# Chunked attention, Fourier mixing and MLP on one core: the first batch's up-projection begun token tile by token tile

## The chip, the cores and the metric

The kernel runs on one core of one Trainium2 chip. The metric is the device time of the whole program in microseconds (us); where several runs are compared, the median counts. All arithmetic is in 32-bit floats; the MLP's weights come in as 64-bit floats and are rounded to 32 bits on the chip.

## The reference

Eight batches of 576 tokens, eight heads of 64. Attention is taken within chunks of 64 tokens; then a two-dimensional Fourier transform whose real part is added, a norm, and an MLP of width 2048 with a Relu.

```python
scores = scale * np.matmul(q_c, k_c.transpose(0, 1, 2, 4, 3))   # per chunk of 64 tokens
scores = scores - np.max(scores, axis=-1, keepdims=True)
attn = np.exp(scores)
attn = attn / (np.sum(attn, axis=-1, keepdims=True) + 1e-09)
x = np.matmul(attn, v_c)                                        # then (B, S, H * D) = (8, 576, 512)
X = np.fft.fft(np.fft.fft(x, axis=1), axis=2)
u = x + np.real(X)
mu = np.mean(u, axis=-1, keepdims=True)
var = np.mean((u - mu) ** 2, axis=-1, keepdims=True)
un = (u - mu) / np.sqrt(var + 1e-06)
out = u + np.maximum(un @ w_ch1, 0.0) @ w_ch2                   # w_ch1 (512, 2048), w_ch2 (2048, 512)
```

## The kernel before, in words

The order of the work on each engine is the order in which the program writes it; nothing is rescheduled. An instruction waits for the data that it needs and for the buffer that it writes to be given up by its last reader, and whatever is written later for the same engine waits behind it.

**Start.** The first batch (b = 0) goes alone, with functions of its own. attention_early does the attention of its five token tiles (four full ones and a rest tile that it shares with batch 1). fourier_early then does its Fourier mixing in three parts, divided by yields: first the products with the sequence tables into z and the middle row mid (L741, L744), which are copied to zf (L751 to L759) and zr (L761 to L767); then the products with the dimension tables into early_xp (L771); then, for each of two pairs of token tiles (low and high), the addition to x (L785, L788, L789), the mean and variance (means: L633 and L634 on VectorE, L637 and L638 on ScalarE, which give rstd), the normalisation (normed, L819 to L825) and the transposition by TensorE and ScalarE (turned: four transposes L329, then the copy L838 into unT). normed works on ScalarE for the first tile (L823, with a shift made by L819 on VectorE) and on VectorE for the other three (L825). keep_warm issues products of a constant tile into a buffer that nobody reads (idle, L1143).

**Rounding the weights.** The weights come in as 32 pieces: four groups of four for w_ch1 (512 hidden features, that is four feature tiles, by 128 input features each, with the group outermost), then those of w_ch2; the pieces are numbered in this order. round_weight(i) does the head of piece i and the tail of piece i - 1. The head ("h" below) is two masks on VectorE (L305, L308) and three steps on ScalarE: fraction (L299) and exponent (L302, L303). The tail ("t") is three steps on VectorE (L317, L318, L319), of which L317 needs L299 and L318 needs L303; it then gives the raw buffer free, and the load of a later piece is issued on SP's queue (L284). Seven raw buffers are filled from the start. round_next calls round_weight for the next piece; attention_early calls it twice, the second time with put_off, a list into which the ScalarE steps are put instead of being issued; the main program issues them after the first part of fourier_early. A third call follows after fourier_early.

**The main loop.** After that, the MLP of batch group after batch group runs step by step, and after each step the loop writes a share of the next batch's attention and Fourier work ("sides"), and then round_next, twice in each of the first four steps. For the first group, up_first walks over four groups f of four feature tiles; for each it takes four PSUM buffers up and sums over the four input pieces kk, with one yield after each kk; after the last kk each up goes through a Relu on ScalarE into h1 (L939). So the step of f and kk needs exactly its own weight piece, the pieces being numbered in the same order. In the third step's share the loop writes the transposes of batch 1's first q and k; in the fourth's, after the first four Relus, its scores (sc, L380), their maximum (L393) and the subtraction (L395).

**PSUM.** ps_t has two buffers of one bank (transposes, z), ps_a one buffer of two banks (the second half of z, and the scores sc), ps_f four buffers of one bank (idle, the two early_xp, mid, later up). A buffer of a pool is taken over when all that used it is through.

Of the kernel before, what the change touches and what calls it, by code (L numbers as in the profile page):

```python
# [8 lines left out]
FP32 = mybir.dt.float32  # L9
# [7 lines left out]
def kernel(  # L17
# [265 lines left out]
            free.remove(fit[0])  # L283
            nc.sync.dma_start(out=raw(i).rearrange("p f r -> p (f r)"), in_=pieces[i][1].bitcast(U32))  # L284

    def round_weight(i, later=None):

        if i < len(pieces):
            w, t = pieces[i][0], raw(i)
            lo, hi, wi = t[:, :, 0], t[:, :, 1], w.bitcast(U32)
            p = power[i] = three_p.tile([128, 512], U32, tag="o", name="power")

            def fraction(w=w, wi=wi):
                nc.scalar.activation(out=w, in_=wi, func=ACTF.Copy, scale=2.0 ** -20, bias=1.0)  # L299

            def exponent(p=p):
                nc.scalar.activation(out=p, in_=p, func=ACTF.Relu, scale=-1.0, bias=top[:, 0:1])  # L302
                nc.scalar.activation(out=p, in_=p, func=ACTF.Relu, scale=-8.0, bias=top[:, 1:2])  # L303

            nc.vector.tensor_scalar(wi, hi, 0x000FFFFF, None, ALU.bitwise_and)  # L305
            if later is None:
                fraction()
            nc.vector.tensor_scalar(p, hi, 0x7FF00000, None, ALU.bitwise_and)  # L308
            if later is None:
                exponent()  # L310
            else:
                later += [fraction, exponent]
        if 0 < i <= len(pieces):
            w, t = pieces[i - 1][0], raw(i - 1)
            lo, hi = t[:, :, 0], t[:, :, 1]
            p = power.pop(i - 1)
            nc.vector.scalar_tensor_tensor(w, lo, 2.0 ** -52, w, ALU.mult, ALU.add)  # L317
            nc.vector.scalar_tensor_tensor(p, hi, 0x80000000, p, ALU.bitwise_and, ALU.bitwise_or)  # L318
# [208 lines left out]
    def attention_early():  # L527

        lo, hi = first[0], first[1] - 1

        def ready(n):
            if n == at[LO, 0, 1]:
                shift_early(0)
            if n == at[HI, 0, 1]:
                fold(0, 1)
            if n == at[HI, 0, 0]:
                fold(0, 0)
            if n + 3 > hi:
                load_v(n + 3)

        att_T(lo)
        att_S(lo)
        for n in range(lo, hi + 1):
            if n < hi:
                att_T(n + 1)
            softmax(n)
            if n > lo:
                att_V(n - 1)
                ready(n - 1)
            if n < hi:  # L550
                att_S(n + 1)
            if n in (lo, hi):
                keep_warm(1)
            att_P(n)
        shift_early(1)
        fold(0, NM)
        keep_warm(1)
        att_V(hi)
        ready(hi)
        keep_warm(6)  # L560
        turn_tables()
        round_next()
        round_next(put_off)

    def attention(b):

# [156 lines left out]
    def fourier_early():  # L723
# [12 lines left out]
        for i in order:  # L736
            at_ = {"start": i == order[0], "stop": i == order[-1], "skip_group_check": True}
            for T in range(4):
                p = slice(0, 128) if i < NM else slice(T % 2 * CH, T % 2 * CH + CH)
                d0_ = T * HQ if i < NM else T // 2 * HQ  # L740
                nc.tensor.matmul(out=z[T][:, 0:NQ], lhsT=pm[i][p, d0_:d0_ + HQ], rhs=tk[p, i, T // 2], **at_)  # L741
            p, d0_ = (slice(0, 128), DM) if i < NM else (slice(CH, 128), 2 * HQ)
            for r, (c0, c1) in enumerate(mids):
                nc.tensor.matmul(  # L744
                    out=mid[32 * r:32 * r + 1, 0:c1 - c0], lhsT=pm[i][p, d0_:d0_ + 1], rhs=tk[p, i, 0, c0:c1], **at_
                )
            if i == order[0]:
                keep_warm(3)
        for T in range(4):
            if T % 2:  # L750
                nc.vector.tensor_copy(zf[:, T, :], z[T][:, 0:NL])  # L751
# [2 lines left out]
        for r, (c0, c1) in enumerate(mids):  # L754
            n, from_ = min(c1, NL) - c0, mid[32 * r:32 * r + 1]
            if r % 2:
                nc.vector.tensor_copy(zf[0:1, 2, c0:c0 + n], from_[:, 0:n])
            else:
                nc.scalar.copy(zf[0:1, 2, c0:c0 + n], from_[:, 0:n])  # L759
        for T in range(4):  # L760
            nc.scalar.copy(zr[:, T, 0, 0:NQ - NL], z[T][:, NL:NQ])  # L761
            upper, mirrored = zr[:, T, 0, NQ - NL:CH], z[T][:, NQ - 2:NL:-1]
            nc.scalar.activation(out=upper, in_=mirrored, func=ACTF.Copy, scale=1.0 if T < 2 else -1.0)
            if T == 2:
                n = NL - c0
                nc.scalar.copy(zr[0:1, T, 0, 0:NQ - NL], from_[:, n:c1 - c0])
                nc.scalar.copy(zr[0:1, T, 0, NQ - NL:CH], from_[:, NQ - 2 - c0:n:-1])  # L767
        yield
        for i in range(NM):
            for T, tab in ((0, cos_d), (1, cos_d), (3, sin_d), (2, sin_d)):  # L770
# [1 line left out]
                    out=early_xp[0][i][:, T % 2::2], lhsT=zf[:, T, 128 * i:128 * (i + 1)], rhs=tab[:, T % 2::2],  # L772
                    start=(T == 0), stop=(T == 2), skip_group_check=True,
                )
        keep_warm(4)
        yield

        def turned_(s):
            keep_warm(2)
            turned(0, s)  # L780

        for i in range(NM):
            y, (low, high) = early_xp[0][i], groups[0][2 * i:2 * i + 2]
# [12 lines left out]
        normed(0, 3)  # L796
        turned_(3)
        yield


# [6 lines left out]
    def normed(g, s):  # L807
        if s >= len(groups[g]):
            return
        n = groups[g][s]  # L810
        if (g, s) == (0, 3):
            un = one_p.tile([128, NJ, 128], FP32, tag="pT", name="un").rearrange("p j t -> p (j t)")
        else:
            un = three_p.tile([128, DM], FP32, tag="o", name="un")
        mean, rstd = sts.pop(n)
        if g == 1 or (g, s) == (0, 0):
            shift_ = sm_p.tile([128, 1], FP32, tag="shift", name="shift")
            if g == 0:
                nc.vector.tensor_scalar(shift_, mean, rstd, -1.0, ALU.mult, ALU.mult)  # L819
            else:  # L820
                nc.scalar.activation(out=shift_, in_=mean, func=ACTF.Copy, scale=-1.0)
                nc.scalar.activation(out=shift_, in_=shift_, func=ACTF.Identity, scale=rstd)
            nc.scalar.activation(out=un, in_=natural(n), func=ACTF.Identity, scale=rstd, bias=shift_)  # L823
        else:
            nc.vector.tensor_scalar(un, natural(n), mean, rstd, ALU.subtract, ALU.mult)  # L825
        uns[g, s] = un
# [95 lines left out]

    def up_first():

        unT = unTs.pop(0)
        h1 = one_p.tile([128, KF, G * 128], FP32, tag="big", name="h1")
        for f in range(0, KF, 4):
            ups = [ps_f.tile([128, G * 128], FP32, tag="ff", name="up") for _ in range(4)]
            for kk in range(KD):
                for m, up in enumerate(ups, f):  # L930
                    nc.tensor.matmul(  # L931
                        out=up,
                        lhsT=w1[:, kk, m * 128:(m + 1) * 128],
                        rhs=unT[:, kk],
                        start=(kk == 0),
                        stop=(kk == KD - 1),
                    )
                    if kk == KD - 1:
                        nc.scalar.activation(out=h1[:, m], in_=up, func=ACTF.Relu)  # L939
                yield h1  # L940

    def up_plain(g):
# [172 lines left out]
    with tc.manual_schedule():  # L1115
# [17 lines left out]
        load_dim_tables()  # L1133
        for i in range(1, len(spaces)):
            load_weight(i)
        n_w = 0
        idle = ps_f.tile([128, 512], FP32, tag="ff", name="idle")
        early_xp = [ps_f.tile([128, 512], FP32, tag="ff", name="early_xp") for _ in range(2)], None

        def keep_warm(times):  # L1140

            for _ in range(times):
                nc.tensor.matmul(out=idle[:, 0:NQ], lhsT=warm[:, 0:128], rhs=warm[:, 0:NQ], start=True, stop=True)  # L1143

        put_off = []

        def round_next(later=None):
            nonlocal n_w
# [125 lines left out]
```

## Time and profile before

| What | Value |
| --- | --- |
| Median of 4 runs | 1103.8 us (1102.77 to 1104.98) |
| The profiled execution: time | 1102.77 us |
| Its span in the profile | 1101.0 us |
| TensorE's busy share of the span | 98% |
| First product of up_first | 52.3 us |

The span reaches from the first instruction of the program to the end of the last; the device time has 1.8 us around it. Times in the views of the profile count from the span's start. PE is TensorE's products, PEld its weight loads, DVE VectorE, ACT ScalarE, POOL GpSimd, SP the engine that issues most transfers; a q behind an engine's name is its queue. A product of 32-bit floats shows as two records, with two weight loads, and a transpose as one. A row of the timeline gives start, duration, engine, line, operation, tiles and count; instructions of one kind that follow each other are merged.

### The profile page before, as it was taken

To read this page: it belongs to the slowest core of one execution; us is meant where nothing else is said; L and a number is where in the kernel's file an instruction comes from. 1 tells how busy PE (TensorE), PEld (TensorE's weight loads), DVE (VectorE), ACT (ScalarE), POOL (GpSimd) and SP (SyncE) were. 2 spreads that over 40 slices of the span, in tenths; PEclk is the share of its full clock that TensorE was granted. 3 is DMA by queue.
4 is the path that set the end of the run, shared out by engine and by line. 5 is a ranking of instruction groups with operands and counts; after the bars stand their busy time and mean duration, and the time that the engine had idled before them with its cause. 6 is when DMAs were issued, how large, how long until landed. Compare 5 with 4: busy or idle time off the path is not lost.

```text
span 1101.0 us, 18766 instructions
## 1 busy us (share of the span) xinstructions
PE 1076.5 (98%) x7016; PEld 846.7 (77%) x7016; DVE 582.8 (53%) x1260; ACT 296.4 (27%) x725; POOL 281.0 (26%) x403
## 2 busy tenths in 40 slices
PE   8999999999999999999999999999999999999998
PEld 6644454447887888888887888888888888888887
DVE  4799987224566355663566455725663534323511
ACT  4688553212112311322022212221123102201200
POOL 4300102354405140243124230424042401220140
PEclk9999999999999999999999999999999999999999
DMA  8767657678566547692669257754753355446232
GB/s 168 236 185 187 155 166 230 183 238 276 197 192 201 154 146 208 188 249 83 194 180 259 88 180 216 207 172 138 205 169 104 117 192 176 127 154 205 82 115 77
DMA packets 147970, 192.73 MB, mean 175 GB/s; under 512 B 66126, under 2 KB 104014, under 8 KB 140712
## 3 DMA queue, kind: packets, MB, share of 16 engines
q1 hardware_dynamic: 145620, 190.20, 57.8%
q8 instruction: 56, 0.92, 0.3%
q0 software_dynamic: 512, 0.68, 0.3%
q10 hardware_dynamic: 1748, 0.66, 0.2%
q14 instruction: 34, 0.28, 0.1%
HBM read 167.22 MB, written 24.12 MB: 174 GB/s over the span
## 4 chain that ended last, share of the span: by engine, by line
PE 82%; DMA 6%; DVE 5%; SPq 2%; ACT 2%; issue 1%; DVEq 0%; ACTq 0%
PE pb L1065 19%; PE pa L1065 15%; PE pb L1015 14%; PE pa L1015 11%; PE dn L969 5%; PE up L948 4%; PE up L931 3%; PE pt L329 3%; DMA q<-in_q_dram 3%; PE more_z L648 2%; PE mix L696 2%; PE z L648 2%; PE xp L428 1%; DMA k<-in_k_dram 1%; PE sc L380 1%
## 5 line engine op out<-in xcount | busy, mean ns | idle before, releaser
L921 POOL TENSOR_TENSOR h<-h 128x256 f32<-128x256 f32 x64 | 56.3, 885 | 274.5 <-PE pb L1015 152.4
L1065 PE MATMUL pa<-wb,h 128*128 128x256 f32 x512 | 115.6, 380 | 0.0
L1065 PE MATMUL pb<-wb,h 128*128 128x256 f32 x512 | 114.9, 379 | 0.0
L1015 PE MATMUL pb<-unT,wa 128*128 128x256 f32 x448 | 107.0, 382 | 4.9 <-DVE wa L1024 4.4
L1015 PE MATMUL pb<-wa 128*128 128x256 f32 x448 | 107.2, 382 | 2.4 <-DVE h L1032 2.4
L1015 PE MATMUL pa<-unT,wa 128*128 128x256 f32 x448 | 106.6, 381 | 0.0
L1065 PEld LDWEIGHTS pa<-wb,h 128*128 128x128 f32 x512 | 96.1, 190 | 13.4 <-issue 0.5
L1065 PEld LDWEIGHTS pb<-wb,h 128*128 128x128 f32 x512 | 96.3, 190 | 12.6
L1015 PEld LDWEIGHTS pb<-unT,wa 128*128 128x128 f32 x448 | 84.0, 190 | 20.5 <-DVE wa L1024 9.4
L1015 PEld LDWEIGHTS pb<-wa 128*128 128x128 f32 x448 | 83.7, 190 | 15.3 <-DVE h L1032 3.6
L1015 PEld LDWEIGHTS pa<-unT,wa 128*128 128x128 f32 x448 | 83.8, 190 | 11.2
L931 PE MATMUL up<-unT,wa 128*128 128x512 f32 x128 | 58.0, 599 | 2.0 <-ACT h L939 1.2
L969 PE MATMUL dn<-wb,h 128*128 128x512 f32 x128 | 57.4, 596 | 1.3 <-ACT h L939 1.3
L1065 PE MATMUL pb<-wb,yall 128*128 128x256 f32 x256 | 58.2, 381 | 0.0
L1065 PE MATMUL pa<-wb,yall 128*128 128x256 f32 x256 | 57.9, 380 | 0.0
L1030 ACT ACTIVATE h<-pa 128x256 f32<-128x256 f32 x56 | 21.5, 384 | 134.8 <-PE pa L1015 134.8
L1065 PE MATMUL pb<-wb 128*128 128x256 f32 x256 | 57.7, 379 | 0.0
L1022 DVE TENSOR_TENSOR wa<-pa,wa 128x256 f32<-128x256 f32 x56 | 23.8, 425 | 62.5 <-PE pa L1015 61.1
L948 PE MATMUL up<-unT,wa 128*128 128x512 f32 x128 | 56.8, 595 | 0.0
L1015 PE MATMUL pa<-wa 128*128 128x256 f32 x224 | 53.4, 381 | 1.5 <-ACT wa L1020 1.5
L1065 PEld LDWEIGHTS pa<-wb,yall 128*128 128x128 f32 x256 | 47.7, 190 | 6.4
L1065 PEld LDWEIGHTS pb<-wb,yall 128*128 128x128 f32 x256 | 47.7, 190 | 6.3
(242 smaller groups left out, 1657.0 us busy)
## 6 DMA issues: line engine op xcount, KB each, us to landing
wb<-s SPq DMA_DIRECT2D x56, 1024.0 KB
wa<-s SPq DMA_DIRECT2D x196, 256.0 KB
xall<-in_moe_w_ch_dram SPq DMA_DIRECT2D x22, 512.0 KB
q<-in_q_dram SPq DMA_DIRECT2D x96, 112.0 KB
k<-in_k_dram SPq DMA_DIRECT2D x96, 112.0 KB
v<-in_v_dram SPq DMA_DIRECT2D x124, 64.0 KB
yall<-in_moe_w_ch_dram SPq DMA_DIRECT2D x10, 512.0 KB
s<-wb SPq DMA_DIRECT2D x20, 256.0 KB
```

The costliest lines, as they stand in the source:

```text
L329: nc.tensor.transpose(pt[:, j, :], src(j), ident)
L380: nc.tensor.matmul(out=sc[t0:t0 + CH, e, j * CH:(j + 1) * CH], lhsT=a[r0:r0 + D, 2 * j + c, 0:CH], rhs=b[r0:r0 + D, 2 * j + c, 0:CH], star ...
L648: nc.tensor.matmul(out=out_, lhsT=lhsT[p], rhs=tk[p, i, T // 2 if T != 5 else 0, cols], start=start, stop=stop, skip_group_check=True,)
L696: nc.tensor.matmul(out=mix[:, cols], lhsT=zt[:, T], rhs=tab, start=(T == 0), stop=(T == 3), skip_group_check=True,)
L921: nc.gpsimd.tensor_tensor(out=h1[:, m, hi], in0=h1[:, m, lo], in1=h1[:, m, hi], op=ALU.subtract)
L931: nc.tensor.matmul(out=up, lhsT=w1[:, kk, m * 128:(m + 1) * 128], rhs=unT[:, kk], start=(kk == 0), stop=(kk == KD - 1),)
L948: nc.tensor.matmul(out=up, lhsT=w1[:, kk, m * 128:(m + 1) * 128], rhs=unT[:, kk], start=(kk == 0), stop=(kk == KD - 1),)
L969: nc.tensor.matmul(out=dn, lhsT=h1[:, m, s * 128:(s + 1) * 128], rhs=w2[:, m, :], start=(m == 0), stop=(m == KF - 1),)
L1015: nc.tensor.matmul(out=dst, lhsT=w[:, kk, r], rhs=rhs[o][:, kk], start=(o in (0, 2) and kk == 0), stop=(kk == 1), skip_group_check=True,)
L1022: nc.vector.tensor_tensor(out=b, in0=dst, in1=a, op=ALU.add)
L1030: nc.scalar.activation(out=h1[:, m, lo], in_=dst, func=ACTF.Relu)
L1065: nc.tensor.matmul(out=dst, lhsT=lhs[:, m], rhs=w[:, m], start=(o in (0, 2) and m == 0), stop=(m == HF - 1), skip_group_check=True,)
```

## The change

- The products of the first four feature tiles (f = 0) with weight piece 0 (kk = 0) are taken out of up_first's first step, which is left with a yield alone, and are written in fourier_early for each of the four token tiles by itself: columns(s), four products of 128 columns. Tiles 0 and 1 are taken after both have been turned, before tile 2 is; tiles 2 and 3 after tile 3.
- Feature tiles 0 and 1 sum in two buffers of ps_f, feature tiles 2 and 3 in the two banks of ps_a. Their Relus keep their order on ScalarE; those of tiles 2 and 3 are written after all four products.
- Token tile 1 is normalised on ScalarE, as tile 0 is, and the shift of both is made on ScalarE too (two short steps), not on VectorE.
- Piece 0's tail is written ahead of piece 1's head. The head of piece 1 goes to after the zf copies; its fraction and the first half of its exponent (L302 of before) are issued after the early_xp products, the second half (L303 of before) after tile 1 is turned.
- Products of keep_warm are dropped: three between the first and the second round of Fourier products, one of the four after early_xp, and all but one of the eight beside turned. What is left of them writes to mid instead of idle.

```diff
-    def round_weight(i, later=None):
-        if i < len(pieces):
+    def round_weight(i, later=None, parts="ht"):
+        if "h" in parts and i < len(pieces):
...
             def exponent(p=p):
                 nc.scalar.activation(out=p, in_=p, func=ACTF.Relu, scale=-1.0, bias=top[:, 0:1])
+
+            def power_(p=p):
                 nc.scalar.activation(out=p, in_=p, func=ACTF.Relu, scale=-8.0, bias=top[:, 1:2])
...
-                later += [fraction, exponent]
-        if 0 < i <= len(pieces):
+                later += [fraction, exponent, power_]
+        if "t" in parts and 0 < i <= len(pieces):
...
         turn_tables()
-        round_next()
-        round_next(put_off)
+        round_weight(0)
+        round_weight(1, parts="t")
...
-            if i == order[0]:
-                keep_warm(3)
...
                 nc.scalar.copy(zf[0:1, 2, c0:c0 + n], from_[:, 0:n])
+        round_weight(1, put_off, "h")
         for T in range(4):
             nc.scalar.copy(zr[:, T, 0, 0:NQ - NL], z[T][:, NL:NQ])
...
-        keep_warm(4)
+        idle[0] = mid
+        for do in put_off[:2]:
+            do()
+        keep_warm(3)
         yield
-
-        def turned_(s):
-            keep_warm(2)
-            turned(0, s)
+        ups = ps_a.tile([128, 2, 512], FP32, tag="att", name="up_a")
+        first_ups.extend([ps_f.tile([128, 512], FP32, tag="ff", name="up") for _ in range(2)])
+        first_ups.extend([ups[:, i] for i in range(2)])
+
+        def columns(s):
+            for m, up in enumerate(first_ups):
+                nc.tensor.matmul(
+                    out=up[:, s * 128:(s + 1) * 128], lhsT=w1[:, 0, m * 128:(m + 1) * 128],
+                    rhs=unTs[0][:, 0, s * 128:(s + 1) * 128], start=(s == 0), stop=False, skip_group_check=True,
+                )
...
-            if i > 0:
+            if i == 0:
+                normed(0, 0)
+            means([high])
+            if i == 0:
                 normed(0, 1)
-                turned_(1)
-            normed(0, 2 * i)
-            means([high])
-            turned_(2 * i)
+                turned(0, 0)
+                keep_warm(1)
+        turned(0, 1)
+        put_off[2]()
+        columns(0)
+        columns(1)
+        normed(0, 2)
+        turned(0, 2)
         normed(0, 3)
-        turned_(3)
+        turned(0, 3)
+        columns(2)
+        columns(3)
         yield
...
-        if g == 1 or (g, s) == (0, 0):
+        if g == 1 or g == 0 and s < 2:
             shift_ = sm_p.tile([128, 1], FP32, tag="shift", name="shift")
-            if g == 0:
-                nc.vector.tensor_scalar(shift_, mean, rstd, -1.0, ALU.mult, ALU.mult)
-            else:
-                nc.scalar.activation(out=shift_, in_=mean, func=ACTF.Copy, scale=-1.0)
-                nc.scalar.activation(out=shift_, in_=shift_, func=ACTF.Identity, scale=rstd)
+            nc.scalar.activation(out=shift_, in_=mean, func=ACTF.Copy, scale=-1.0)
+            nc.scalar.activation(out=shift_, in_=shift_, func=ACTF.Identity, scale=rstd)
...
-            ups = [ps_f.tile([128, G * 128], FP32, tag="ff", name="up") for _ in range(4)]
+            ups = first_ups if f == 0 else [ps_f.tile([128, G * 128], FP32, tag="ff", name="up") for _ in range(4)]
             for kk in range(KD):
-                for m, up in enumerate(ups, f):
+                for m, up in enumerate(ups, f) if f + kk > 0 else ():
...
-                    if kk == KD - 1:
+                    if kk == KD - 1 and (f > 0 or m < 2):
                         nc.scalar.activation(out=h1[:, m], in_=up, func=ACTF.Relu)
+                if kk == KD - 1 and f == 0:
+                    for m in (2, 3):
+                        nc.scalar.activation(out=h1[:, m], in_=ups[m], func=ACTF.Relu)
                 yield h1
...
-        n_w = 0
-        idle = ps_f.tile([128, 512], FP32, tag="ff", name="idle")
+        n_w = 2
+        idle = [ps_f.tile([128, 512], FP32, tag="ff", name="idle")]
...
         for step, _ in enumerate(fourier_early()):
             if step == 0:
                 turn_dim_tables()
-                for do in put_off:
-                    do()
         round_next()
```

More of the change, by code (lines that the diff above doesn't have):

```diff
@@ L310, in round_weight @@
                 exponent()
+                power_()
             else:
-                later += [fraction, exponent]
-        if 0 < i <= len(pieces):
+                later += [fraction, exponent, power_]
+        if "t" in parts and 0 < i <= len(pieces):
             w, t = pieces[i - 1][0], raw(i - 1)
@@ L936, in up_first @@
                         stop=(kk == KD - 1),
+                        skip_group_check=True,
                     )
-                    if kk == KD - 1:
+                    if kk == KD - 1 and (f > 0 or m < 2):
                         nc.scalar.activation(out=h1[:, m], in_=up, func=ACTF.Relu)
+                if kk == KD - 1 and f == 0:
+                    for m in (2, 3):
+                        nc.scalar.activation(out=h1[:, m], in_=ups[m], func=ACTF.Relu)
                 yield h1
@@ L1142, in keep_warm @@
             for _ in range(times):
-                nc.tensor.matmul(out=idle[:, 0:NQ], lhsT=warm[:, 0:128], rhs=warm[:, 0:NQ], start=True, stop=True)
-        put_off = []
+                nc.tensor.matmul(out=idle[0][:, 0:NQ], lhsT=warm[:, 0:128], rhs=warm[:, 0:NQ], start=True, stop=True)
+        put_off, first_ups = [], []
         def round_next(later=None):
```

## The prediction

> **What bounds the kernel now.** I read the page first (TensorE busy 98% of the span), then the chain of waits, then the timeline of the first 90 us, since the diff touches only what runs before about 70 us. From the first up-projection on, the chain is TensorE; from the page's engine sums:
>
> ```profile
> PE 1076.5 (98%) x7016; PEld 846.7 (77%) x7016; DVE 582.8 (53%) x1260; ACT 296.4 (27%) x725; POOL 281.0 (26%) x403
> ```
>
> and from the chain of waits (start, duration, what; a line such as L931 is the source line):
>
> ```profile
> 52.29 10.57 PE up L931 x24
> 62.85 0.87 PE pt L329 x8
> 63.73 3.44 PE up L931 x8
> 67.16 0.66 PE sc L380 x32
> 67.82 0.53 issue
> 68.35 0.59 ACT h L939
> 68.94 0.04 issue
> 68.98 3.70 PE up L931 x8
> ```
>
> A product of 512 columns leaves two records, 3.44/8 = 0.43 us each, so one step of up_first (one weight piece, four feature tiles) takes 3.44 us. Four steps and eight transposes run without a stop, and then TensorE stands 1.2 us. The timeline says for what:
>
> ```profile
> 49.89 0.55 DVE L825 TENSOR_SCALAR un<-xall,st,rstd 128x512 f32<-128x512 f32 x1 [0.60 <-ACT rstd L638]
> 50.35 0.42 DVE L305 TENSOR_SCALAR wa<-xall 128x512 uint32<-128x512 uint32 x1
> ...
> 52.13 0.63 ACT L299 ACTIVATE wa<-wa 128x512 f32<-128x512 uint32 x1
> ...
> 54.23 0.69 DVE L318 SCALAR_TENSOR_TENSOR power<-xall,power 128x512 uint32<-128x512 uint32 x1
> ...
> 67.72 0.72 ACT L303 ACTIVATE power<-power,top 128x512 uint32<-128x512 uint32 x1
> ...
> 68.35 2.04 ACT L939 ACTIVATE h<-up 128x512 f32<-128x512 f32 x4
> ...
> 68.98 3.70 PE L931 MATMUL up<-unT,wa 128*128 128x512 f32 x8 [1.19 <-ACT h L939]
> ```
>
> The four Relus of the first four feature tiles stand on ScalarE behind the rounding of weight piece 8. Rounding is paced by VectorE: 2.61 us for a piece (L305 at 50.35, 52.95, 55.56 and so on to 65.99), without a gap. So the first four tiles end early or late for nothing: **the second four start when the rounding, begun at 50.35, lets the Relus through.** Later, VectorE waits 1.12 us at 81.56 for the next scores and all follows TensorE again; a shift of the second four's start is therefore carried to the end.
>
> **What the Trainium skill says.** "Perfetto Trace Analysis", section "Tensor Engine Instruction (MATMUL, LD_WEIGHTS)", calls ScalarE and VectorE strict FIFO; the Relus above agree, their sums were done at 67.2. "TensorE: Matmul & The Clock Gate", section "LDWEIGHTS (loading the stationary operand)", gives columns/1.2 ns, 107 for 128; the trace has 190 ns for 128 columns and 80 for one, 110 for the columns. Its section "What's actually happening" says that TensorE falls to half clock after an idle window of about 3.4 us and returns after a busy one, the windows running freely. The trace shows the return at its start, and no gap over 1.5 us later, so it can't show a fall:
>
> ```profile
> 1.23 6.16 PEld L1143 LDWEIGHTS idle<-warm 128*128 128x128 f32 x16 [1.23 <-DVE more_v L1124]
> ...
> 43.02 2.85 PEld L1143 LDWEIGHTS idle<-warm 128*128 128x128 f32 x12
> ```
>
> Sixteen would take 3.8 us at the later pace; the cold start cost 2.4.
>
> **The change, part by part.**
>
> 1. *Fourier start.* Three keep_warm (six records, 34.27 to 35.59) go: the Fourier products come 1.3 us sooner. On VectorE, piece 1's masks waited for their DMA until 36.51, and piece 0's rounding behind them held the zf copies to 39.49. Now piece 0 is finished at about 37.1 (L318 when L303 ends at 35.69, then 0.72 and 0.7), and the copies follow TensorE at 37.6. The four row copies, which take turns between ScalarE and VectorE, end at 39.5 (41.0 before); piece 1's two masks (0.68 us) fit before the first half of early_xp is there. The first add (L785) starts at 40.2 (41.63): -1.4.
>
> 2. *VectorE.* Per pair of token tiles, start to start: add 0.73, statistics 0.73, 0.10, add 0.57, 0.19, statistics 0.72, 0.10: 3.14, twice 6.28, to 46.5. The shift of L819 and its 0.44 us wait are gone. The norms of tiles 2 and 3 stay here; the second waits for rstd of tile 3 until 47.1 and takes 0.46. Rounding of piece 2 starts at **47.6** (50.35).
>
> 3. *ScalarE.* Two norms are here now. By the rows of a later group each is 0.22 + 0.33 for the shift and 0.72 for un. Fraction and exponent of piece 1 go at 40.4 to 41.7, before rstd is due. In order: un 0 ends 43.7, un 1 45.4, unT 0 copied 45.3 to 45.9, four short rstd steps up to 47.05 (the last statistics end at 46.54), unT 1 47.05 to 47.65, power of piece 1 to 48.2.
>
> 4. *TensorE.* Sixteen products of 128 columns are 32 records at 0.107 (transposes and the 110 ns above), 3.44 us: what the four dropped products took. Tile 0's 0.86 us hides behind waiting; tile 1's runs 47.7 to 48.55; the transposes of tiles 2 and 3 stand behind it to 49.4; ScalarE copies unT 2 and 3 from 49.2 to 50.3; tile 2's products run meanwhile, tile 3's to 51.6. The second piece starts at 51.6 (55.73): **-4.1 us**. The first four tiles end at 51.6 + 3 x 3.44 + 0.87 = 62.8 (67.16).
>
> 5. *Rounding.* ScalarE's fraction of piece 2 stands behind the copy of unT 3: 50.16 (52.13), its power ends at 52.16, and VectorE's L318 on it starts at 52.2 (54.23). So the rounding gains 2.0, not 2.75, and the Relus start at 66.3 (68.35).
>
> 6. *The added wait.* Feature tiles 2 and 3 now sum in the two banks of ps_a, a pool of one buffer, which the next scores (L380, in program order before the second four) take over. They wait for the Relus of tiles 2 and 3: three more at 0.49 and the last one's 0.59, to 66.3 + 2.1 = **68.4**; 0.63 us of scores follow. Behind them stands all of TensorE, and VectorE's maximum (L393 at 68.60, now 69.1) with pieces 9 and 10. The second four start at **69.03 against 68.98: +0.05 us.** VectorE's half microsecond is inside its 1.12 us wait at 81.56.
>
> 7. *TensorE idles* from 62.8 to 68.4, 5.6 us. A free-running window of 3.4 us fits wholly in that in about two of three phases. I charge the price seen at the start, **+2.4 us** (0 if the gate stays open; 3.4 is an estimate from the page, two windows at half rate).
>
> At nothing: piece 7's load, freed a little sooner, still stands on SP's queue behind v's issues (39.91 to 50.85) and is used after 60; POOL's dim tables wait for their DMA as before; the other dropped keep_warm ran beside waits, and the longest gap they leave is about 1 us.
>
> Sum: +0.05 + 2.4 = **+2.45 us**. The profiled execution took 1102.77 (span 1101.0 and 1.8 around it), 1.0 under the median: 1105.2 on its scale, 1106.2 on the median's.
>
> **The rivals.**
>
> - *The gate stays open.* All else as above: +0.05 +- 0.6, 1103.9. For it: nothing in this trace shows a fall. Against: the gap is longer than the window.
> - *Faster: the scores aren't held.* If their banks are free at 62.8, the second four's first two tiles start at 63.5 in free ps_f banks and the third waits for the first Relu, 66.9 against 70.7: -3.8, 1100.0. It decides as soon as the Relus of tiles 2 and 3 are through before about 66. Against it: one buffer, and the Relus' place in ScalarE's queue. A rounding that starts over 2 us sooner than worked out would do the same on a smaller scale.
> - *The columns are paced by weight loads at 190 ns.* Then tile 1's products end 0.65 later, and so do the copies of unT 2 and 3 and the Relus: +0.7, with the closed gate +3.1, 1106.9. A gate that closes already among the norms, for want of keep_warm, does the same: TensorE's own slowness is hidden by the 5.6 us, but the transposes come late. Against: weight loads at 52.28 start 0.11 apart.
> - That the change doesn't do what it says: the same arithmetic is issued in other places; I see nothing left undone.
>
> **How the numbers follow.** 0.2% is 2.2 us, about what a measurement of this kernel can tell from no change. Closed gate 0.50 (0.45 over 2.2, 0.05 within), slow columns 0.13 (slower), open gate 0.27 (same), faster 0.10: faster 0.10, same 0.32, slower 0.58. Range: 1101.8 (an open gate with a rounding 2 us better) to 1108.0 (3.4 for the gate, 0.7 for the columns), leaving out most of the faster case and a little above.
>
> **What would show it.** L305 of piece 2 near 47.6, L931 at 51.6, the Relus near 66.3, L380 near 68.4 with over 5 us of idle on ps_a's account, and then L931 records 0.86 instead of 0.43 us apart for some 3 to 5 us. If L380 starts before 66, steps 5 and 6 are wrong; if the records stay at 0.43, step 7 is.

## The result, and the profile after

| | before | after |
| --- | --- | --- |
| Median | 1102.95 us (62 runs) | 1105.49 us (41 runs) |
| Ratio, 95% interval | | 1.0022 [1.0017, 1.0027] |
| Profiled execution, its span | 1102.77, 1101.0 us | 1105.53, 1103.8 us |
| Mean granted TensorE clock | 0.999 | 0.996 |

The change makes the kernel slower by 2.4 us (1.9 to 3.0 by the interval). TensorE's useful work is the same: 22 records of useless products are gone, and eight records of 512 columns have become 32 of 128. The page of after has

```profile
PE 1074.1 (97%) x7018; PEld 846.0 (77%) x7018; DVE 583.1 (53%) x1258; ACT 297.6 (27%) x730; POOL 280.6 (25%) x403
```

with 2.4 us less of TensorE busy in a span that is 2.8 us longer. The chain of waits of after (start, duration, what) shows where it stands:

```profile
60.73 1.72 PE up L951 x4
62.44 1.72 PE up_a L951 x4
64.16 5.38 issue
69.53 1.13 PE sc L383 x32
70.67 5.60 PE up L951 x8
76.27 0.87 PE pt L332 x8
77.14 3.44 PE up L951 x8
```

The first four feature tiles are through at 64.16, sooner than in before (67.16, and that with a Fourier start 1 us later here, see below). Then nothing for 5.38 us, scores that take 1.13 instead of 0.66 us, and a step of four products (eight records) that takes 5.60 instead of 3.70. The timeline says what the scores waited for:

```profile
48.63 0.42 DVE L307 TENSOR_SCALAR wa<-xall 128x512 uint32<-128x512 uint32 x1
51.25 0.65 ACT L299 ACTIVATE wa<-wa 128x512 f32<-128x512 uint32 x1
53.29 0.69 DVE L321 SCALAR_TENSOR_TENSOR power<-xall,power 128x512 uint32<-128x512 uint32 x1 [0.67 <-ACT power L305]
...
66.77 0.72 ACT L305 ACTIVATE power<-power,top 128x512 uint32<-128x512 uint32 x1
67.40 1.06 ACT L960 ACTIVATE h<-up 128x512 f32<-128x512 f32 x2
68.35 1.08 ACT L963 ACTIVATE h<-up_a 128x512 f32<-128x512 f32 x2
69.53 1.13 PE L383 MATMUL sc<-kT,qT 64*64 64x64 f32 x32 [5.38 <-issue]
```

L963 are the Relus of feature tiles 2 and 3, which sum in ps_a; the scores (L383) take over ps_a when the last of them ends at 69.43. The view calls the idle time "issue" (it names nothing that ended it); that the scores start 0.1 us after that end tells what it was, and so does the same wait in the experiment with ps_a held, where it bears the Relu's name. In the windows (stretch, length, then busy time of PE, PEld, DVE, ACT, POOL; third from the end the mean of the granted clock, 1.00 for full and 0.50 for half) the clock falls while TensorE stands:

```profile
66.00:67.00 1.00, 0.00 (x0) 0.00 (x0) 0.99 (x2) 0.97 (x3) 0.00 (x0) 1.00 0.02 4
67.00:68.00 1.00, 0.00 (x0) 0.00 (x0) 0.69 (x1) 1.00 (x3) 0.00 (x0) 0.89 0.00 0
68.00:69.00 1.00, 0.00 (x0) 0.00 (x0) 0.00 (x0) 1.00 (x3) 0.00 (x0) 0.50 0.91 233
...
74.00:75.00 1.00, 1.00 (x3) 0.52 (x2) 0.96 (x4) 0.69 (x1) 0.00 (x0) 0.70 0.02 8
75.00:76.00 1.00, 1.00 (x3) 0.34 (x3) 1.00 (x4) 0.89 (x2) 0.00 (x0) 1.00 0.98 246
```

A mean of 0.89 in the microsecond from 67 and of 0.70 in that from 74 put the stretch at half clock at about 67.8 to 74.6. It covers the scores and the first five records of the second four.

### The profile page after: what moved, and what is told of

It is laid out like the page before. It is cut to its first block, busy times and chain, and to the rows that moved or that the text cites. A ratio compares the mean times of both kernels' runs of the same rounds, so it can differ in the third digit from the quotient of the medians.

```text
span 1103.8 us, 18775 instructions
## 1 busy us (share of the span) xinstructions
PE 1074.1 (97%) x7018; PEld 846.0 (77%) x7018; DVE 583.1 (53%) x1258; ACT 297.6 (27%) x730; POOL 280.6 (25%) x403
## 4 chain that ended last, share of the span: by engine, by line
PE 86%; DVE 6%; ACT 2%; DMA 2%; issue 2%; SPq 1%; POOL 1%; DVEq 0%; ACTq 0%; POOLq 0%
PE pb L1089 20%; PE pa L1089 15%; PE pb L1039 14%; PE pa L1039 12%; PE dn L993 5%; PE up L972 4%; PE pt L332 3%; PE up L951 3%; PE more_z L651 2%; PE mix L699 2%; PE z L651 2%; PE xp L431 2%; PE sc L383 1%; DMA q<-in_q_dram 1%; DMA wa<-s 1%
## 5 line engine op out<-in xcount | busy, mean ns | idle before, releaser
L972 PE MATMUL up<-unT,wa 128*128 128x512 f32 x128 | 56.8, 595 | 0.0
L716 POOL TENSOR_TENSOR xall<-y,xall 128x513 f32<-128x513 f32 x14 | 21.3, 1520 | 123.7 <-DVE y L710 123.7
```

Source lines behind the costliest of these rows:

```text
L972: nc.tensor.matmul(out=up, lhsT=w1[:, kk, m * 128:(m + 1) * 128], rhs=unT[:, kk], start=(kk == 0), stop=(kk == KD - 1),)
```

## The experiments

**Theory**: the early products open a gap that costs in two ways, the hold of ps_a (which eats what the faster start gains) and the clock gate (TensorE falls to half clock: the gate "closes"); the start and the norms are a gain. **Rivals**: the gate isn't the cause; or the early products cost something else (late transposes and copies); or the gain of the start is not there at all. All ratios are to before, with 95% intervals; 0.001 is 1.1 us. The kernels were run in three groups, each on one chip beside before: the gap filled, two tiles early, none early and the hold; the three with the Relus ahead and the first trial of two tiles with the gap filled; the last four.

Since the Fourier start falls sooner or later from trace to trace and moves everything up to 90 us, the traces are compared from the first z (L741 of before, L744 of after), in us after it:

| | first z at | piece 2's rounding | first Relu | second four | ratio |
| --- | --- | --- | --- | --- | --- |
| before | 31.92 | 18.43 | 36.43 | 37.06 | 1 |
| after | 32.91 | 15.72 | 34.49 | 37.68 | 1.0022 [1.0017, 1.0027] |
| after, gap filled (e1) | 32.14 | 15.72 | 34.49 | 37.30 | 1.0005 [0.9996, 1.0013] |
| two tiles early (e3) | 31.97 | 15.71 | 34.92 | 35.55 | 0.9993 [0.9986, 1.0] |
| none early (e4) | 31.95 | 15.71 | 34.75 | 35.37 | 0.9972 [0.9963, 0.9981] |
| none early, again (e10) | 32.56 | 15.72 | 33.69 | 34.31 | 0.9975 [0.9964, 0.9987] |
| two early, gap filled (e11) | 32.97 | 15.70 | 34.02 | 34.65 | 0.9976 [0.9966, 0.9987] |
| start alone (e12) | 31.52 | 16.95 | 34.94 | 35.57 | 0.9992 [0.9984, 0.9999] |
| before, ps_a held (e5) | 32.52 | 18.42 | 36.40 | 39.21 | 1.0035 [1.0022, 1.0047] |

That the first Relu comes later in e3 than in e11, and later in e4 than in e10, belongs to a stretch at half clock among the norms of the traces e3 and e4 (below).

### The gap, filled

After, with eight useless products behind the Relus' place in the program, into a buffer of ps_t that nobody reads:

```diff
                     for m in (2, 3):
                         nc.scalar.activation(out=h1[:, m], in_=ups[m], func=ACTF.Relu)
+                    spare = ps_t.tile([128, 512], FP32, tag="pt", name="spare")
+                    for _ in range(8):
+                        nc.tensor.matmul(out=spare[:, 0:NQ], lhsT=warm[:, 0:128], rhs=warm[:, 0:NQ],
+                                         start=True, stop=True)
```

> The changed kernel, with eight useless keep_warm products (sixteen records, 3.9 us) behind the first four feature tiles, in the gap in which TensorE waits for the scores' banks. Theory (the gap lets the clock gate close): the second four feature tiles start when they did (70.6 in the changed kernel's profile, give or take 1 us of the start), but the granted clock stays at 1.00 and the records are 0.43 us apart, not 0.86: 2.1 us less than the changed kernel, 1103.4, ratio to before 1.0003. Rival (the slow records come of something else, such as a busy memory): they stay 0.86 apart, 1105.5, ratio 1.0022.

Measured: 1102.95 us, ratio 1.0005 [0.9996, 1.0013], clock 1.00 in every window from 62 to 78 us. Its chain of waits:

```profile
66.63 1.06 ACT h L960 x2
67.70 0.98 ACT h L963 x2
68.68 0.14 issue
68.81 0.69 PE sc L383 x32
69.51 3.63 PE up L951 x8
```

The Relus and the hold are as in after (34.49 from z in both), the scores take 0.69 and the step 3.63 us. So the gate is worth 1.0022 - 1.0005, 1.9 us by the ratios, give or take 1.1, and with it gone the kernel is no faster than before: the hold alone eats the gain.

### The hold, by itself

Before, with its feature tiles 2 and 3 in ps_a and their Relus last, nothing else changed:

```diff
-            ups = [ps_f.tile(...) for _ in range(4)]
+            ups = [ps_f.tile(...) for _ in range(2 if f == 0 else 4)]
+            if f == 0:
+                both_ = ps_a.tile([128, 2, 512], FP32, tag="att", name="up_a")
+                ups += [both_[:, i] for i in range(2)]
...
```

The window in the expectation is the one of about 3.4 us in the prediction's step 7.

> The kernel before with one part of the change alone: the first four feature tiles sum in two buffers of ps_f and the two banks of ps_a, and the Relus of tiles 2 and 3 are written after all four products. Theory: the scores wait for the last of four Relus, 68.35 + 2.1 = 70.4, and the second four start at 71.1 instead of 69.0: +2.1 us if the gate stays open. TensorE then stands 3.3 us, just under the window, so the gate is open in some or all runs: 1105.1, ratio 1.0019; with a closed gate up to 1107.2. Rival (the hold is harmless): 1103.0, ratio 1.000.

Measured: 1106.85 us, ratio 1.0035 [1.0022, 1.0047]. Timeline and windows:

```profile
71.10 0.69 PE L380 MATMUL sc<-kT,qT 64*64 64x64 f32 x32 [3.34 <-ACT h L945]
71.73 5.40 PE L934 MATMUL up<-unT,wa 128*128 128x512 f32 x8
```

```profile
70.00:72.00 2.00, 0.90 (x33) 0.86 (x34) 0.14 (x1) 0.96 (x2) 0.00 (x0) 1.00 0.68 215
72.00:74.00 2.00, 2.00 (x3) 0.70 (x3) 1.97 (x5) 0.69 (x2) 0.00 (x0) 0.51 0.04 8
74.00:76.00 2.00, 2.00 (x4) 0.87 (x3) 1.97 (x4) 1.79 (x3) 0.00 (x0) 0.64 0.00 0
```

The Relus come where they came (36.40 and 36.43 from z), the second four 2.15 us later: three Relus and the scores, which before had slipped in ahead of the Relus. That is the price of the hold. The gate closes too, after a gap of 3.34 us and only when TensorE is working again (from about 72). The 2.15 us and the slow step's 1.70 (5.40 for 3.70) make 3.85; the ratio gives 3.9.

### No early products, or two tiles of them

Two kernels keep the rest of the change. One takes feature tiles 0 and 1 alone token tile by token tile, and leaves ps_a free; the other takes none early (the first_ups.extend that stays in this diff goes too). In both, all four Relus follow their products again, as in before.

```diff
-        ups = ps_a.tile([128, 2, 512], FP32, tag="att", name="up_a")
         first_ups.extend([ps_f.tile(...) for _ in range(2)])
-        first_ups.extend([ups[:, i] for i in range(2)])
...
-            ups = first_ups if f == 0 else [ps_f.tile(...) for _ in range(4)]
+            old = first_ups if f == 0 else []
+            ups = old + [ps_f.tile(...) for _ in range(4 - len(old))]
...
-                for m, up in enumerate(ups, f) if f + kk > 0 else ():
+                for m, up in list(enumerate(ups, f))[len(old) if kk == 0 else 0:]:
...
```

> The changed kernel, but only feature tiles 0 and 1 are taken token tile by token tile; feature tiles 2 and 3 take two buffers of ps_f in up_first as before, so ps_a is free for the scores. Theory (the hold of ps_a costs twice, by its own wait and by the gate): the second four start one Relu (0.63 us) after the first Relu begins, at about 68.0, 2.6 sooner than in the changed kernel, and at full clock: 4.7 us less, 1100.8, ratio 0.998. Rival (the loss lies with ScalarE's extra norms or the later rounding): the hold is without effect, 1105.5 as it was.

> The changed kernel without the products taken token tile by token tile: all of the first four feature tiles' products with piece 0 stand in up_first, in ps_f, as before; the moved rounding, the norms on ScalarE and the dropped keep_warm stay. Theory (the second four's start is set by rounding and Relus, not by how early the first four are done): the first four end at about 66.5 to 67, still before the first Relu is through at 68.0, so the time is that of the kernel with two feature tiles within 0.5 us, 1100.8 to 1101.3, ratio 0.998. Rival (the early products are worth TensorE's time): 1.7 to 3.4 us more than with two feature tiles.

Measured: two tiles 1101.56 us, 0.9993 [0.9986, 1.0]; none 1099.46 us, 0.9972 [0.9963, 0.9981]. With ps_a free, both start the second four 0.62 us behind the first Relu, as before does. The two-tile kernel's timeline and windows:

```profile
67.52 5.40 PE L950 MATMUL up<-unT,wa 128*128 128x512 f32 x8 [2.06 <-ACT h L959]
```

```profile
68.00:70.00 2.00, 2.00 (x5) 0.73 (x4) 2.00 (x5) 2.00 (x5) 0.00 (x0) 0.67 0.66 211
70.00:72.00 2.00, 2.00 (x4) 0.97 (x3) 1.97 (x5) 1.79 (x3) 0.00 (x0) 0.50 0.23 72
```

A gap of 2.06 us closed the gate here. Of the two-tile kernel's 21 runs, nine had a mean clock of 0.999 and a median of 1100.5 us, twelve a clock of 0.996 to 0.998 and a median of 1102.8 us. The clock also falls in the last microseconds of most traces, which takes up to 0.001 off the mean (2.5 us at half clock in before); a stretch of 3.4 us at half clock takes 0.0015. The mean doesn't say where in a run the clock was low, and this trace has a second low stretch among the norms, from 48.2 to 51.6. The trace of the kernel without early products has one too, from 49.2 to 52.6. No single gap on TensorE is longer than about 1 us there, but there are several. Such a stretch makes transposes late, in e3 those of unT, in e4 those of batch 1's q and k behind the slow first steps of up_first. The rounding stands on ScalarE behind their copies, so the first Relu comes later from z, by 0.9 us in e3 against e11 and by 1.1 in e4 against e10. So the mean clock alone doesn't show that the gap is to blame in the twelve slow runs. With the gap filled (below) 5 of 28 runs have a mean of 0.998 or lower, against 12 of 21 here, and this points to the gap.

The kernel without early products leaves a gap of 0.94 us there. Its eleven runs don't show that the stretch among the norms costs it time: the four at a mean of 0.998 or lower have a median of 1099.1 us, the seven others 1099.5.

### Is it the gap alone?

The two-tile kernel with three useless products in its gap (the edit of the first experiment, with 3 for 8) should then equal the one that takes none early. It was first run without that one beside it:

> The kernel with two feature tiles taken token tile by token tile, with three useless keep_warm products (1.5 us) behind the first four feature tiles, ahead of the scores. In its profile without them TensorE stood 2.1 us at 65.5 and ran at half clock from 68.6 to 72, so 2.1 us may be enough for the gate. Theory (the gate is the whole difference to the kernel without early products, 1099.5): the second four start at 67.5 as before, the clock stays at 1.00 there, 1099.5, ratio 0.9972. Rival (the early products cost something else as well): 1101.6 still, ratio 0.9993.

Measured: 1101.60 us, 0.9985 [0.9976, 0.9993]; a gain, but a smaller one than expected, and it was open whether early products cost anything besides. So both ran on one chip:

> The changed kernel without the products taken tile by tile (all of f = 0 in up_first, in ps_f), the other parts of the change kept; run beside the next one so that the two can be compared on one chip. Expected: ratio to before near 0.997 (about 1100.0 us), second four feature tiles at 67.3 us, as this design gave before; if it comes out at 0.9985 or above, the gain is smaller than it seemed.

> Feature tiles 0 and 1 taken tile by tile, all of 2 and 3 in up_first, and three useless products in the gap ahead of the second four; beside the kernel that takes none early. Theory (early products cost nothing but the gap that they open, which closes the clock gate): equal to that kernel within 0.5 us, ratio near 0.997. Rival (the early products also delay the transposes and copies of the last two token tiles, and with them the rounding): slower than it by 1 to 1.5 us, ratio near 0.9985, and the second four at 67.8 with the Fourier products at the same time.

Measured: none early 1099.99 us, 0.9975 [0.9964, 0.9987]; two early with the gap filled 1100.73 us, 0.9976 [0.9966, 0.9987]. By these ratios they are equal, as the theory had it. The rival's mechanism is there in the traces, at 0.33 us (first Relu at 34.02 against 33.69 from z). Its 1 to 1.5 us is not seen in this pair, but the intervals leave room for some 1 us, and the first trials (0.9985 with the gap filled, 0.9972 with none early) lie on that side; so early products may cost a little besides the gap. In the chain of waits of the kernel without early products, TensorE waits for nothing but the rounding:

```profile
64.34 0.63 ACT wa L299
64.97 0.62 ACT power L302
...
66.25 0.58 ACT h L958
66.83 0.04 issue
66.87 3.70 PE up L949 x8
```

### Where the gain is from: the start alone, and the useless products

Before, with the moved rounding of pieces 0 and 1 and without three keep_warm; norms, shift and the keep_warm beside turned as before:

```diff
-        round_next()
-        round_next(put_off)
+        round_weight(0)
+        round_weight(1, parts="t")
...
-            if i == order[0]:
-                keep_warm(3)
...
+        round_weight(1, put_off, "h")
```

> The kernel before with the start of the change alone: piece 0's tail ahead of piece 1's head, the head of piece 1 after the zf copies, and three useless products dropped between the rounds of Fourier products; the norms, VectorE's shift, the products beside turned and the MLP as before. Theory (the moved rounding and the earlier Fourier products carry part of the gain, the norms on ScalarE the rest): second four feature tiles near 67.6 us (from 69.0), ratio near 0.9987, between before and the kernel without early products (0.997). Rival (the norms carry all of it): second four at 68.6 to 69.0, ratio 1.000. Second rival (the start carries all of it): second four at 67.3, ratio 0.997.

Measured: 1101.82 us, 0.9992 [0.9984, 0.9999]. Piece 2's rounding starts at 16.95 from z, 1.48 sooner than in before; with norms and the rest of the change it is 15.72, 1.23 more. In the traces both carry the gain, as the theory had it; by the ratios the start alone gives 0.9 us (0.1 to 1.8) of some 2.8. The second four's 67.1 us is below the 67.6 expected, because this trace's Fourier start was 0.4 us sooner.

None early, with two useless products ahead of each of the four turned, as before:

```diff
+                keep_warm(2)
                 turned(0, 0)
-                keep_warm(1)
+        keep_warm(2)
         turned(0, 1)                                                  # and so ahead of tiles 2 and 3
```

> The changed kernel without the products taken tile by tile, and with two useless products ahead of each of the four turned, as in the kernel before. The design without them runs TensorE at half clock from 49 to 53 us. Theory (the slow stretch is hidden, and the idle time that it fills is what keeps the gate open before the second four): the first four end some 2 us sooner, at about 64, TensorE then stands 2.5 to 3 us, the gate closes in part of the runs, and the second four still start at 67.3: ratio 0.9975 to 0.999, never better than without the useless products. Rival (the slow stretch costs time, the transposes coming late): ratio 0.996 or lower, second four at 66.8 or sooner.

Measured: 1101.04 us, 0.9979 [0.997, 0.9989], not to be told from 0.9975 without them. Half of the expectation missed: the first four don't end at 64, since with the useless products the first step of up_first starts at 50.69, against 49.89 in the trace without them (0.23 of this is a later Fourier start). The gap is 1.12 us, and the gate stays open in this trace. The useless products may keep it open among the norms more often: 3 of these 14 runs have a mean clock of 0.998 or lower, against 9 of 20 in the two trials without them. In time, dropping them is neither a measurable loss nor a gain.

### The Relus ahead of the rounding

Three kernels put the rounding of pieces 7 and 8 behind the first four's Relus: after, the two-tile kernel, and before.

```diff
+                if t == 4:
+                    round_next()
+                    round_next()
...
-                if not heavy:
+                if not heavy and t != 3:
```

> The changed kernel with weight pieces 7 and 8 rounded after the first four feature tiles' Relus are written, not ahead of them: the hold of ps_a stays, but the Relus no longer stand behind rounding. Theory: the first Relu starts when its sums are done, at about 63, the scores at 65.3 and the second four at 66, 3.4 us sooner than in the changed kernel with warm products; TensorE stands some 2.2 us, so the gate may close as it did with two feature tiles: 1099.5 (open) to 1101.6 (closed), ratio 0.997 to 0.999. Rival (the hold alone, not the Relus' place in the queue, makes the delay): 1105.5.

> Two feature tiles taken token tile by token tile, ps_a free, and pieces 7 and 8 rounded after the first Relus. Theory: the first four end at 65.0 to 65.5, the scores run at once, and the second four start one Relu later, at about 66.2; no gap over 1 us, so no closed gate there: 1098.3, ratio 0.996. Rival (the rounding put off for two pieces is missed later, since VectorE then waits for ScalarE behind the Relus): nothing gained on the kernel without early products, 1099.5 or more.

> The kernel before with this alone: pieces 7 and 8 are rounded after the first four feature tiles' Relus. Theory (the Relus' place behind the rounding is the 1.2 us wait at 67.8): the second four start at 67.9, 1.1 us sooner: 1101.6, ratio 0.999. Rival (the rounding put off is missed later): 1102.7 or more, ratio 1.000 or above.

Measured: after with it 1100.65 us, 0.9979 [0.9971, 0.9987]; two tiles with it 1102.09 us, 0.9986 [0.9977, 0.9996]; before with it 1105.28 us, 1.0018 [1.001, 1.0027]. In after the hold stays, but ends early: the scores start at 65.15 after a gap of 1.22 us, at full clock. That confirms from the other side that the Relus' place in ScalarE's queue makes the gap. But the rounding is missed a few microseconds later (timeline of after with the Relus ahead):

```profile
65.78 3.70 PE L951 MATMUL up<-unT,wa 128*128 128x512 f32 x8
...
73.95 0.72 ACT L305 ACTIVATE power<-power,top 128x512 uint32<-128x512 uint32 x1
74.58 0.57 ACT L362 COPY qT<-pt 128x512 f32<-128x512 f32 x1
...
75.20 0.65 PE L332 MATMUL pt<-ident,ex 128*128 128x128 f32 x4 [1.42 <-ACT qT L362]
```

The copies that free ps_t (L362, L371) now stand behind the put-off rounding, and TensorE's next transposes wait for them: 1.42 us here, 2.23 us in the other two. In the trace of before with the Relus ahead the gate then closes, from 78.5; in that of the two-tile kernel, after a gap of the same length, it doesn't. For two tiles the theory's number missed and the rival's held: the wait had been moved, not removed. In before it costs more than it brings.

## Why the prediction was right

It gave +2.45 us on the profiled execution's scale and slower as likeliest; measured are +2.4 by the ratio and +2.76 in the profiled runs. The mechanism was right, a gain at the start that is eaten by the hold of ps_a, and a gate that closes in the gap; that the sum met the number so closely is in part luck, as steps 6 and 7 show. Step by step, with the 0.99 us of the Fourier start taken off the times of after:

| Step | predicted | measured | less 0.99 |
| --- | --- | --- | --- |
| 1 first add | 40.2 | 41.23 | 40.24 |
| 2 piece 2's rounding | 47.6 | 48.63 | 47.64 |
| 4 second piece | 51.6 | 52.82 | 51.83 |
| 4 first four end | 62.8 | 64.16 | 63.17 |
| 5 first Relu | 66.3 | 67.40 | 66.41 |
| 6 scores start | 68.4 | 69.53 | 68.54 |
| 6 second four | 69.03 | 70.59 | 69.60 |

**Steps 1, 2, 3 and 5** held within about 0.1 us; for step 3's queue on ScalarE, the fraction of piece 2 (L299) starts at 51.25 and L321 at 53.29, with 0.99 off at 50.26 and 52.30, for 50.16 and 52.2. Step 5's argument, that ScalarE's copies of unT 2 and 3 let 0.75 us of the rounding's 2.75 slip, is what the experiments show: without early products the first Relu comes 2.74 us sooner from z than in before (33.69 in e10, where the clock stays full among the norms, against 36.43), with them 1.94.

**Step 4** was 0.2 to 0.4 short; it lay inside the gap and cost nothing.

**Step 6**, the hold, held to 0.14 us at the start of the scores. The second four come 0.57 late against 69.03: 0.14 is that start, 0.43 is step 7, since the scores at half clock take 1.13 us for 0.69. With the gap filled they come at 37.30 from z, 0.24 later than in before, for a predicted 0.05.

**Step 7** took +2.4 us for the gate. Against the kernel with the gap filled it cost 0.4 on the scores and 2.0 on the second four (5.60 for 3.63), 2.4 in this trace, and 1.9 us by the two ratios. But the price came from the slow start of the program, and that it fits is partly luck: in the traces with ps_a held and with two tiles early the same fall cost 1.70 us. The low stretch was shorter there, 3.4 us; here it lasted 6.8, of which a quarter was spent waiting. The 3.4 us that the prediction estimated from two windows was too much as a cost.

The chance was too low. The working asked for a window that fits wholly into 5.6 us, two of three phases; in fact the gate fell in practically every run (all but three had a mean clock of 0.997 or lower, those three 0.998; before mostly 0.999 to 1.0), and far shorter gaps do it. "TensorE: Matmul & The Clock Gate", section "What's actually happening" in the Trainium skill, asks for an idle window of about 3.4 us. The length agrees with these traces, the idleness doesn't: a gap of 3.34 us closed the gate in the profiled execution (and all five runs of that kernel have the low mean clock), and one of 2.06 us did, so in this case a window need not have been idle throughout. About half was enough, as the last section works out. A gap of 5.38 us, however it falls on windows of 3.41, leaves at most 0.7 us of work in one of them.

What the prediction put at nothing, the other dropped keep_warm with gaps of about 1 us, cost nothing in the trace of after, where the clock is full until 67.8. But in e3 and e4, which drop the same products, the clock fell among the norms.

**What the sum left out.** Against the second score stage (80.79 in before), after is 3.58 us late: 0.99 of start, 0.19 of hold (the predicted 0.05 and the 0.14 of step 6) and 2.4 of gate. It ends 2.76 late, since one wait further on gives part back, with a later one taking some again. Before, then after, ahead of the scores near 230 us:

```profile
226.64 0.70 PE L428 MATMUL xp<-v,pT 64*64 64x65 f32 x32
227.65 1.08 DVE L348 STREAM_TRANSPOSE kT<-k 128x512 f32<-128x512 f32 x1 [6.43 <-DMA k<-in_k_dram]
228.79 0.69 PE L380 MATMUL sc<-kT,qT 64*64 64x64 f32 x32 [1.45 <-DVE rd L441]
```

```profile
230.13 0.70 PE L431 MATMUL xp<-v,pT 64*64 64x65 f32 x32
231.03 0.70 PE L383 MATMUL sc<-kT,qT 64*64 64x64 f32 x32 [0.21 <-DVE kT L351]
```

In before TensorE stands 1.45 us for k (VectorE's transposition into kT waits for it, and the short rd stands behind that), whose load was issued on SP's queue at 222.71, 3.9 us before L428; in after it was issued at 224.86, 5.3 us before. 1.3 us come back there. The traces with the changed start give back 0.5 to 1.7 us at this place, before with the Relus ahead 1.1, and before with ps_a held 0.1. Near 706 us, 1.1 us are lost again in after, between 0 and 1.5 in the others. Why SP's queue stands better there was not tried. In the profiled executions the terms that the sum didn't have nearly cancel (start +0.99, 1.3 and 0.5 given back near 229 and 477 us, 1.1 lost near 706); how they average over all runs is not known, so +2.45 meets +2.4 more closely than its working deserves.

**The rivals.** The open gate (1103.9, ratio 1.000) is what the filled gap gives, 1.0005: the rival's size was right, but its condition, an open gate, was not met. The faster case needed the Relus of tiles 2 and 3 through before 66; with the Relus put ahead they are (scores at 65.15), and the kernel is faster, by 2.3 us instead of 3.8, since the moved rounding is missed later. The columns were not paced by weight loads at 190 ns: four records of 128 columns take 0.45 us in after, 0.11 each. A gate that closes among the norms, named beside that rival, is what e3 and e4 show; in e3 the transposes come late, as it said. The trace of after doesn't show it.

**The better kernel** is the change without its early products: 0.9972 and 0.9975 in its two trials, some 3 us under before and 5 under after. Two tiles early with the gap filled may be as good (0.9985 and 0.9976).

## What to carry to other kernels

A stage that is made shorter ahead of a fixed due time only lengthens the wait there. Ask which buffer the early result occupies meanwhile, who is next in it, and whether the engine will stand long enough to lose its clock; in these traces a gap of two microseconds on TensorE, or several of up to one in a row, was already enough for that where it took half of a window. An order that lets a late consumer through sooner has to be paid by what it overtakes on the same queue; look at the next thing that this queue owes.

## What the hardware showed

- In the clock record of each trace the changes lie whole multiples of 3.41 us apart. Five stretches at half clock lasted 3.4 us (two in e3, one each in e4, ps_a held, and before with the Relus ahead), the one in after 6.8. At half clock a record of 512 columns takes 0.85 us instead of 0.43, so 3.4 us full of such work cost 1.70 us (5.40 for 3.70).
- Cut each trace into windows of 3.41 us in step with these changes. Away from the first and the last 10 us of the program, the six windows ahead of a fall have this much work on TensorE: 0.00 us (after, 64.36 to 67.77), 0.93 (ps_a held, 68.62 to 72.03), 1.20 (before with the Relus ahead, 75.07 to 78.49), 1.35 (two tiles, 65.25 to 68.66), 1.68 (none early, 45.73 to 49.14) and 1.83 (two tiles, 44.77 to 48.18). At full clock, no window of the fourteen traces with more than 1.83 us was followed by a fall, nor were two with 1.68 and 1.81. So here the gate closed when about half of a window was idle, in one gap or in several.
- It follows that the length of a gap doesn't decide alone. The 2.23 us in before with the Relus ahead lie in one window, and the clock fell, 0.7 us after TensorE had begun to work again. In the two-tile kernel the same 2.23 us are divided over two windows (1.84 us of work in the first, 71.95 to 75.37), and it didn't.
- The first products of the Fourier transform start anywhere from 31.5 to 33.6 us in fourteen traces, each time 0.1 us after ScalarE has copied the tables (tk); in eleven of them these copies had waited for a DMA, up to 1.68 us. The four traces with the old norms lie at 31.5 to 32.5, the ten others at 31.9 to 33.6. With one trace for each kernel this can't be told from chance, and whether part of it belongs to the change is left open.
